# Gated linear attention in halves of 64 tokens with the state inside the output matmul, and a feed-forward block behind it

## The chip, the cores and the metric

The kernel runs on one core of a Trainium2 chip. A core has five engines that work side by side, each through its own instructions in order: PE (TensorE, matmuls, with its weight loads shown apart as PEld), DVE (VectorE), ACT (ScalarE), POOL (GpSimd) and SP (SyncE, which here issues DMAs). Matmuls write to PSUM; DVE and ACT can read it[...]. The metric is the time of one execution in microseconds on the device.

## The reference

There are 4 batches, 8 heads, 768 tokens and a head size of 48; d_model is 8 x 48 = 384. Everything is 32-bit floating point, except the two weight matrices, which arrive as 64-bit numbers.

```
state = alpha[t, :, None] * state + k[t] outer v[t]     # per batch and head, 48 x 48
y[t]  = q[t] @ state
x     = y, heads side by side                           # (4, 768, 384)
xn    = (x - mean(x)) / sqrt(var(x) + 1e-6) * g_ln
out   = x + max(xn @ w_ch1, 0) @ w_ch2                  # 384 -> 1536 -> 384
```

The recurrence runs over all tokens. In a block of tokens it can be written with matmuls. With L the running sum of log(alpha) from the block's start, q times exp(L) is matched against k times exp(-L), entries with a later key are cleared, and the result multiplies v. The state from before the block enters as (q times exp(L)) @ state. At the block's end the state is (state + (k exp(-L))^T v) times exp(L of the last token), here called the gate.

## The kernel before, in words

The tokens are cut in 6 chunks of 128; a chunk of one batch is a block, so there are 24 blocks. The generator `attention(c, b)` (L242) computes one block, step by step; each `yield` ends a turn. Its turns are:

- `la`, the logarithm on ACT (L246); `lps`, the running sum as a matmul with a triangle of ones (L249); two exponentials on ACT, `ek` and `eq` (L253, L254)
- k times `ek` on POOL (L256), q times `eq` on DVE (L258); a DMA writes the last row of `eq` to DRAM (`row`, L262), and a later one reads it back as a column per head (`gate`, L294)
- transposes of q and k on PE (`tps`, L272), copied out of PSUM to `qkT` by ACT or DVE (L276, L278); heads 2p and 2p+1 are a pair and sit in partitions 0 to 47 and 64 to 111
- scores `aps` (L285) on PE, copied to `at` by DVE with the triangle as mask (L289), so that cleared entries stay zero
- output `yps`: the scores times v (L307), and from the second chunk on q times the state, accumulated into the same place (L302); copied to `x` by ACT (L311) and kept in DRAM (L314)
- sums for the state, `sps` (L321), added to `st` by DVE (L326) and multiplied by the gate on POOL (L331)
- mean and variance on DVE (L335, L336), `rstd` on ACT (L338, L339), the normalised `xn` on DVE (L342), its transpose `xps` on PE (L349), copied to `xT` by ACT (L351)

The feed-forward part takes a chunk of all four batches together. Chunk 0 uses plain matmuls (`hidden`, L372, and `project`, L384). The other chunks use schemes that need fewer products and more sums: 15 products per half of the hidden layer (`hidden_product`, L612), with sums of inputs (`combine_x`, L588), and 20 products for the output (`product`, L455), with sums of hidden values (`combine_hidden`, L442). The sums of weights are made once on POOL: `combine_first` (L565) for the first matrix and `combine_weights` (L415) for the second. The weights come in 12 pieces of 768 KB; `take_weights` rounds each to 32 bits with DVE and ACT (L168 to L184). Gains `g_ln` are multiplied into the first matrix there.

The order of all this is written out: in the string `ORDER` each character is one turn. Letters a to x are the 24 blocks, A to L the weight pieces, M the feed-forward matmuls with what empties their PSUM tiles, S the sums of weights, X and N the sums of inputs and hidden values, R the rectifier, O loads of the kept `x`. Every engine gets its instructions in this order, so an instruction that waits holds all later ones of its engine.

All loads of attention and of weights are issued by SP (L121, L156). PSUM has three pools of tiles that matter: tag "a" with three buffers (`lps`, `tps`, `aps`), tag "s" with two (`yps`, `sps`, `xps`), tag "m" with three (feed-forward).

## Time and profile before

| | |
|---|---|
| three runs | 475.37, 476.41 and 476.61 us, median 476.41 |
| profiled execution, span | 472.3 us |
| that span below the median | 4.1 us |
| clock granted to TensorE | 1.000 |
| DMA | 43.29 MB, 92 GB/s in the mean |
| first hidden matmul (L372) | 47.31 us after the start |

The span runs from the first to the last instruction of the one execution that was profiled; what lies around it is not in it, so sums over rows are compared with 472.3 and not with the median. The page gives per engine the time it was busy and, per group of instructions, line, engine, operation, the tile written and the tiles read, the shapes, the number, the total and mean duration, and the idle time before with what ended it. A 32-bit matmul is two passes, so its group counts twice the calls in the code; a transpose is one. Durations of passes overlap: the mean of a row is longer than the distance from one to the next, and for PE's own rate the distance counts.

### The profile page before, as it was taken

How to read it: one execution, taken by the hardware profiler on the slowest of the kernel's cores; microseconds unless marked ns; L12 is line 12 of the kernel's file. 1: busy time of each engine (PE TensorE's matmuls, PEld its weight loads, DVE VectorE, ACT ScalarE, POOL GpSimd, SP SyncE). 2: the span in 40 equal slices, each digit the busy share in tenths (PEclk: the TensorE clock that was granted, in tenths of full speed). 3: DMA queues.
4: the chain of work that ended last, by engine and by line, in shares of the span. 5: the costliest groups of instructions: out<-in, count | busy, mean ns of one | idle time of the engine just before them, and what ended most of it. 6: DMA issues, size and time to landing. Idle time of an engine off the chain costs nothing.

```text
span 472.3 us, 9365 instructions
## 1 busy us (share of the span) xinstructions
PE 457.1 (97%) x3690; PEld 384.5 (81%) x3690; DVE 356.6 (76%) x662; ACT 152.9 (32%) x335; POOL 222.7 (47%) x222
## 2 busy tenths in 40 slices
PE   7899999999999999999999999999999999998996
PEld 5768465567688889998898998898998899987896
DVE  3799899867377799876788867688677579765673
ACT  4576354511033523124342121543031341223300
POOL 4142103069969990727461426460435360544513
PEclk9999999999999999999999999999999999999999
DMA  8986856403301422240331231330020110210001
GB/s 260 334 248 196 282 157 224 123 19 102 85 17 52 129 75 67 70 118 15 104 101 52 86 102 51 83 101 1 34 81 23 35 35 0 80 56 0 1 18 51
DMA packets 40132, 43.29 MB, mean 92 GB/s; under 512 B 13956, under 2 KB 36228, under 8 KB 40088
## 3 DMA queue, kind: packets, MB, share of 16 engines
q1 hardware_dynamic: 39544, 42.56, 29.4%
q8 instruction: 29, 0.48, 0.4%
q10 hardware_dynamic: 544, 0.13, 0.1%
q14 instruction: 15, 0.12, 0.1%
HBM read 33.20 MB, written 9.48 MB: 90 GB/s over the span
## 4 chain that ended last, share of the span: by engine, by line
PE 85%; DVE 5%; POOL 4%; ACT 2%; DMA 2%; issue 2%; POOLq 0%; DVEq 0%; ACTq 0%
PE ops L455 24%; PE hps L612 24%; PE hps L372 7%; PE ops L384 7%; PE aps L285 5%; PE yps L307 4%; PE tps L272 4%; PE yps L302 4%; PE lps L249 3%; PE sps L321 2%; PE xps L349 2%; DMA rk<-in_k_dram 1%; DVE at L289 1%; DVE sum L588 1%; DMA ra<-in_alpha_dram 1%
## 5 line engine op out<-in xcount | busy, mean ns | idle before, releaser
L471 POOL TENSOR_TENSOR ob<-ob,u 128x192 f32<-128x192 f32 x40 | 27.5, 699 | 83.3 <-DVE ob L468 63.9
L612 PE MATMUL hps<-sum,w 128*128 128x256 f32 x240 | 59.9, 382 | 1.1 <-DVE hT L655 1.1
L612 PEld LDWEIGHTS hps<-sum,w 128*128 128x128 f32 x240 | 44.7, 190 | 7.9 <-DVE hT L655 1.5
L455 PE MATMUL ops<-w,hT 128*128 128x192 f32 x280 | 49.6, 328 | 0.0
L664 ACT ACTIVATE hT<-hT 128x512 f32<-128x512 f32 x60 | 36.3, 628 | 35.6 <-POOL hT L634 21.3
L455 PEld LDWEIGHTS ops<-w,hT 128*128 128x128 f32 x280 | 45.7, 190 | 1.1
L331 POOL TENSOR_TENSOR st<-st,gate 128x384 f32<-128x384 f32 x20 | 19.1, 959 | 53.6 <-DVE st L326 44.3
L631 POOL TENSOR_TENSOR hT<-hT,u 128x512 f32<-128x512 f32 x10 | 12.9, 1287 | 56.9 <-DVE u L630 56.9
L256 POOL TENSOR_TENSOR qk<-rk,ek 128x384 f32<-128x384 f32 x22 | 23.3, 1059 | 30.0 <-PE sps L321 12.6
L307 PE MATMUL yps<-rv,at 128*64 128x48 f32 x768 | 36.5, 219 | 0.1
L289 DVE COPY_PREDICATED at<-consts,aps 128x512 f32<-128x512 int32 x48 | 32.2, 724 | 3.6 <-PE aps L285 3.2
L307 PEld LDWEIGHTS yps<-rv,at 128*64 128x64 f32 x768 | 32.9, 138 | 0.6 <-DVE at L289 0.3
L372 PE MATMUL hps<-xT,w 128*128 128x512 f32 x72 | 32.4, 597 | 0.0
L384 PE MATMUL ops<-w,hT 128*128 128x384 f32 x96 | 32.2, 488 | 0.0
L612 PE MATMUL hps<-xT,w 128*128 128x256 f32 x120 | 31.1, 382 | 0.9 <-DVE hT L644 0.9
L285 PE MATMUL aps<-qkT 48*128 48x128 f32 x384 | 28.6, 285 | 2.1 <-DVE at L289 1.3
L285 PEld LDWEIGHTS aps<-qkT 48*128 48x128 f32 x384 | 23.8, 187 | 8.0 <-issue 4.0
L302 PE MATMUL yps<-st,qkT 112*64 112x96 f32 x320 | 29.8, 257 | 0.0
L455 PE MATMUL ops<-ws,sum 128*128 128x192 f32 x160 | 28.9, 328 | 0.7 <-DVE sum L442 0.7
L455 PE MATMUL ops<-ws,hT 128*128 128x192 f32 x160 | 29.5, 327 | 0.0
L276 ACT COPY qkT<-tps 112x512 f32<-112x512 f32 x32 | 18.2, 597 | 29.0 <-PE tps L272 25.7
L455 PEld LDWEIGHTS ops<-ws,sum 128*128 128x128 f32 x160 | 26.3, 190 | 1.4 <-DVE sum L442 1.0
(141 smaller groups left out, 1020.9 us busy)
## 6 DMA issues: line engine op xcount, KB each, us to landing
ws<-in_moe_w_ch_dram SPq DMA_DIRECT2D x12, 768.0 KB, 6.1
ra<-in_alpha_dram SPq DMA_DIRECT2D x24, 192.0 KB, 2.6
rk<-in_k_dram SPq DMA_DIRECT2D x24, 192.0 KB, 3.4
rq<-in_q_dram SPq DMA_DIRECT2D x24, 192.0 KB
rv<-in_v_dram SPq DMA_DIRECT2D x24, 192.0 KB, 2.8
kept<-x SPq DMA_DIRECT2D x24, 192.0 KB, 1.9
ob<-kept SPq DMA_DIRECT2D x24, 192.0 KB, 2.9
out_dram<-ob SPq DMA_DIRECT2D x19, 192.0 KB, 1.9
```

The lines of the kernel that those rows point to most:

```text
L256: nc.gpsimd.tensor_mul(qk[:, 1, :, :D], raws.pop(("k", c, b)), ek)
L285: nc.tensor.matmul(aps[i][:, p], qkT[rows, 1, p], qkT[rows, 0, p], start=True, stop=True)
L289: nc.vector.copy_predicated(out=at[:, i], data=aps[i], mask=mask.unsqueeze(1).broadcast_to([P, NP, P]))
L302: nc.tensor.matmul(yps[s, p].rearrange("p a b -> p (a b)"), qkT[:, 0, p, s], sts[b][:R, p].rearrange("p a b -> p (a b)"), start=True, stop ...
L307: nc.tensor.matmul(yps[s, p, i], at[:, i, p, s], vt[:, 2 * p + i], start=(c == 0), stop=(c == 0 or i == 1))
L331: nc.gpsimd.tensor_mul(st, st, gate.unsqueeze(2).broadcast_to([P, NP, 2 * D]))
L372: nc.tensor.matmul(hps, w1[:, f, j * P:(j + 1) * P], xT_of[c][:, f], start=(f == 0), stop=(f == NF - 1))
L384: nc.tensor.matmul(ops_of[b], hT_of[c][:, j, b], w2[:, j], start=(j == 0), stop=(j == NJ - 1))
L455: nc.tensor.matmul(acc, lhs[:, j], rhs[:, j], start=(j == 0), stop=(j == NT - 1))
L471: getattr(nc.gpsimd, f"tensor_{op}")(x, x, y)
L612: nc.tensor.matmul(acc[:, i], w, b, start=True, stop=True)
L664: nc.scalar.activation(out=x, in_=x, func=AFT.Relu)
```

## The change

Attention works on a chunk of 128 tokens as two halves of 64, each with its own running sum (`upto` has two triangles on its diagonal). Heads p and p+4 form a pair. The scores are computed inside each half only (`aps`, 64 keys by 64 queries). They land in the 64 partitions of `at` that the transposed q of that head does not use; ACT copies q's transpose to the other ones (in two copies), and a separate `kT` holds k's. Beside v, the tile `va` holds the state in the partitions that match q's, so that one matmul per head and half gives scores times v plus q times state. `va` holds all of v in half tiles, and `rv` half of it a second time, in six loads for two batches. The sums for the state, `ups`, are made per half: DVE adds them, POOL multiplies by the half's gate (`gate` has two columns per pair), and ACT copies the state to the next half's place (`carry`, four small copies per block in all). The last chunk now needs a first half's sums and gate too.

exp(-L) is written back to PSUM, and k's product with it moves from POOL to DVE. The normalised `xn` moves from DVE to POOL. The gains are applied when `xT` is copied, in three copies with a scale per partition, and no longer in the weights. `combine_weights` moves from POOL to DVE and gets its own letter W. Loads of alpha, k, q and v take two batches at a time, those of k, q and v of the first chunk inside the blocks' turns; from the middle on `load_one` takes single blocks. Loads of weights go to ACT's queue, and the first three are issued in turns of their own. The string `ORDER` is another one; its extra letters at the end of a generator do nothing.

```diff
--- before.py
+++ after.py
...
-    "babdabcdcabadcbacabbdabaabacababdabacbdbccbadAccdddcBcCedfeacbacaeBeffcgbaededbe"
...
+    "aabBaaaaababbdbaaaabbbBddaaBaaAabbbacceacCdccaabbdbbbcceeeedfebbbaccccacdbAbdcAc"
...
-    raw = ctx.enter_context(tc.tile_pool(name="raw", bufs=B))
+    raw = ctx.enter_context(tc.tile_pool(name="raw", bufs=B // 2))
...
+    HS = P // 2
+    halves = [slice(HS * s, HS * s + HS) for s in range(2)]
...
-    upto = (r[None, :] >= r[:, None]).astype(np.float32)
+    upto = ((r[None, :] >= r[:, None]) & (r[None, :] // HS == r[:, None] // HS)).astype(np.float32)
...
-    def load(c, b, names="akqv"):
-        for n, src in (("a", alpha), ("k", k), ("q", q), ("v", v)):
...
-            t = raw.tile([P, H, D], FP32, name=f"r{n}", tag=f"r{n}",
...
-            nc.sync.dma_start(t, src[b, c * P:(c + 1) * P])
-            raws[n, c, b] = t
+    def load(c, m, names):
+        bs = range(2 * m, 2 * m + 2)
+        rows = slice(c * P, (c + 1) * P)
+        for n, src in (("a", alpha), ("k", k), ("q", q)):
+            if n in names:
+                t = raw.tile([P, 2, 2, NP, D], FP32, name=f"r{n}", tag=f"r{n}")
+                nc.sync.dma_start(t.rearrange("t b i p d -> t b (i p d)"),
+                                  src[bs.start:bs.stop, rows].rearrange("b t h d -> t b (h d)"))
+                raws.update({(n, c, b): t[:, b - bs.start] for b in bs})
+        if "v" in names:
+            rv = raw.tile([P, 2, NP, D], FP32, name="rv", tag="rv")
+            va = raw.tile([P, 2, 2, 2, NP, D], FP32, name="va", tag="va")
+            src = v[bs.start:bs.stop, rows].rearrange("b (s t) (i p) d -> i s t b (p d)", s=2, i=2)
+            for i in range(2):
+                nc.sync.dma_start(rv[halves[i]].rearrange("t b p d -> t b (p d)"), src[i, i])
+                for s in range(2):
+                    nc.sync.dma_start(va[halves[1 - i], :, s, i].rearrange("t b p d -> t b (p d)"),
+                                      src[i, s])
+            for b in bs:
+                raws["v", c, b] = rv[:, b - bs.start], va[:, b - bs.start]
+    lone = {}
+    def load_one(n):
+        c, b = divmod(n, B)
+        for n, src in (("a", alpha), ("k", k), ("q", q)):
+            if n not in lone:
+                lone[n] = raw.tile([P, 2, 2, NP, D], FP32, name=f"r{n}", tag=f"r{n}")
+            t = raws[n, c, b] = lone[n][:, b % 2]
+            nc.sync.dma_start(t.rearrange("t i p d -> t (i p d)"),
+                              src[b, c * P:(c + 1) * P].rearrange("t h d -> t (h d)"))
...
-    for names in ("a", "kq", "v"):
-        for b in range(B):
-            load(0, b, names)
+    for m in range(B // 2):
+        load(0, m, "a")
...
     def load_weights(i):
...
-        nc.sync.dma_start(dst, src)
+        nc.scalar.dma_start(dst, src)
     def round_weights(i):
...
-        if not gains:
-            stt(out=dst, in0=dst, scalar=2.0 ** -20, in1=hi.bitcast(FP32),
-                op0=AOP.mult, op1=AOP.mult)
-            return
-        for f in range(NF):
-            stt(out=dst[:, f], in0=dst[:, f], scalar=g20[:, f:f + 1],
-                in1=hi[:, f].bitcast(FP32), op0=AOP.mult, op1=AOP.mult)
+        stt(out=dst, in0=dst, scalar=2.0 ** -20, in1=hi.bitcast(FP32), op0=AOP.mult, op1=AOP.mult)
     def take_weights(i):
+        if i < STAGED:
+            load_weights(i)
+            yield
...
-        elif pieces[i][2]:
-            for f in range(NF):
-                nc.vector.tensor_scalar_mul(pieces[i][0][:, f], pieces[i][0][:, f],
-                                            g_col[:, f:f + 1])
...
-    for i in range(STAGED):
-        load_weights(i)
...
-    sts = [cpool.tile([P, NP, 2, D], FP32, name=f"st{b}") for b in range(B)]
+    sts = [cpool.tile([R, NP, D], FP32, name=f"st{b}") for b in range(B)]
...
-    ats = [cpool.tile([P, 2, NP, P], FP32, name=f"at{i}") for i in range(2)]
+    ats = [cpool.tile([P, NP, 2, 2, HS], FP32, name=f"at{i}") for i in range(2)]
...
     def attention(c, b):
-        qk = qk_of(c, b).rearrange("p i a b c -> p i (a b) c")
-        eq = eq_of(c, b).rearrange("p a b c -> p (a b) c")[:, :, :D]
-        la = work.tile([P, H, D], FP32, name="la", tag="la")
+        if c == 0 and b % 2 == 0:
+            load(0, b // 2, "kq")
+            yield
+            load(0, b // 2, "v")
+            for i in range(2):
+                for d in range(2):
+                    nc.gpsimd.memset(raws["v", 0, b + d][1][halves[i], 0, i], 0.0)
+            yield
+        qk = qk_of(c, b).rearrange("t n p i c -> t n i p c")[:, :, :, :, :D]
+        eq = eq_of(c, b).rearrange("t p i c -> t i p c")[:, :, :, :D]
+        la = work.tile([P, 2, NP, D], FP32, name="la", tag="la")
...
-        lv = lps[:, :DM].rearrange("p (h d) -> p h d", d=D)
-        ek = work.tile([P, H, D], FP32, name="ek", tag="ek")
-        nc.scalar.activation(out=ek, in_=lv, func=AFT.Exp, scale=-1.0)
+        lv = lps[:, :DM].rearrange("t (i p d) -> t i p d", i=2, d=D)
...
-        yield
-        nc.gpsimd.tensor_mul(qk[:, 1, :, :D], raws.pop(("k", c, b)), ek)
-        yield
-        nc.vector.tensor_mul(qk[:, 0, :, :D], raws.pop(("q", c, b)), eq)
-        if c + 1 < NCB:
-            row = dram.tile([1, NP, P], FP32, name="row", tag="row")
-            gate = work.tile([P, NP], FP32, name="gate", tag="gate", bufs=B)
-            nc.sync.dma_start(row, eq_of(c, b)[P - 1:P].rearrange("o a b c -> o a (b c)"))
-        yield
-        n = c * B + b + (B if c < 2 else B // 2)
-        if c < 2 or 3 * B <= n < NCB * B:
-            load(*divmod(n, B), "akq")
-        yield
-        qkT = work.tile([R, 2, NP, P], FP32, name="qkT", tag="qkT", bufs=2)
+        nc.scalar.activation(out=lv, in_=lv, func=AFT.Exp, scale=-1.0)
+        yield
+        nc.vector.tensor_mul(qk[:, 1], raws.pop(("k", c, b)), lv)
+        yield
+        nc.vector.tensor_mul(qk[:, 0], raws.pop(("q", c, b)), eq)
+        row = dram.tile([2, NP, P], FP32, name="row", tag="row")
+        gate = work.tile([P, 2, NP], FP32, name="gate", tag="gate", bufs=B)
+        nc.sync.dma_start(row, eq_of(c, b)[HS - 1::HS].rearrange("o a b c -> o a (b c)"))
+        yield
+        n = c * B + b + 2
+        if c < 2 and b % 2:
+            load(c + 1, b // 2, "akq")
+        elif n == 3 * B + 1:
+            load_one(n - 1)
+            load_one(n)
+        elif 3 * B + 1 < n < NCB * B:
+            load_one(n)
+        yield
+        at = ats[b % len(ats)]
+        kT = work.tile([R, NP, 2, HS], FP32, name="kT", tag="kT", bufs=2)
+        rows = [slice(0, 64), slice(64, R)]
...
-            if i == 0 or c < 2:
-                nc.scalar.copy(out=qkT[:, i], in_=tps)
+            tv = tps.rearrange("r p (s t) -> r p s t", s=2)
+            if i == 0:
+                for j in range(2):
+                    nc.scalar.copy(out=at[rows[j], :, j], in_=tv[rows[j]])
...
-                nc.vector.tensor_copy(out=qkT[:, i], in_=tps)
-            yield
-        at = ats[b % len(ats)]
-        aps = [ps.tile([P, NP, P], FP32, name=f"aps{i}", tag="a", bufs=3) for i in range(2)]
+                (nc.vector.tensor_copy if c == 0 else nc.scalar.copy)(out=kT, in_=tv)
+            yield
+        aps = [ps.tile([P, NP, 2, HS], FP32, name=f"aps{i}", tag="a", bufs=3) for i in range(2)]
+        for p in range(NP):
+            for s in range(2):
+                for i in range(2):
+                    rs = slice(64 * i, 64 * i + D)
+                    nc.tensor.matmul(aps[i][halves[1 - i], p, s], kT[rs, p, s], at[rs, p, i, s],
+                                     start=True, stop=True)
+        yield
+        for i in range(2):
+            h = halves[1 - i]
+            nc.vector.copy_predicated(
+                out=at[h, :, i], data=aps[i][h],
+                mask=mask[h, h].unsqueeze(1).unsqueeze(1).broadcast_to([HS, NP, 2, HS]))
+        yield
+        with nc.allow_non_contiguous_dma(reason="two rows to columns"):
+            nc.sync.dma_start(gate, row.rearrange("o a c -> c o a"))
+        yield
+        rv, va = raws.pop(("v", c, b))
+        heads = [slice(0, 64), slice(64, R)]
+        last = c + 1 == NCB
+        ups = [ps.tile([R, NP, D], FP32, name=f"ups{s}", tag="s") for s in range(1 if last else 2)]
+        for p in range(NP):
+            for s, up in enumerate(ups):
+                for i, h in enumerate(heads):
+                    vs = rv[halves[s], p] if s == i else va[halves[s], s, i, p]
+                    nc.tensor.matmul(up[h, p], qk_of(c, b)[halves[s], 1, p, i, :h.stop - h.start],
+                                     vs, start=True, stop=True)
+        yield
+        st = sts[b]
+        def carry(s, to):
+            for i, h in enumerate(heads):
+                nc.scalar.copy(out=to[h, s, i], in_=st[h])
+        for s, up in enumerate(ups):
+            nc.vector.tensor_add(st, up, st)
+            yield
+            nc.gpsimd.tensor_mul(st, st, gate[:R, s].unsqueeze(2).broadcast_to([R, NP, D]))
+            yield
+            if s == 0:
+                carry(1, va)
+                yield
+        yps = ps.tile([P, 2, NP, D], FP32, name="yps", tag="s")
...
-                rows = slice(64 * i, 64 * i + D)
-                nc.tensor.matmul(aps[i][:, p], qkT[rows, 1, p], qkT[rows, 0, p],
-                                 start=True, stop=True)
-        yield
-        for i in range(2):
-            nc.vector.copy_predicated(out=at[:, i], data=aps[i],
-                                      mask=mask.unsqueeze(1).broadcast_to([P, NP, P]))
-        yield
-        if c + 1 < NCB:
-            with nc.allow_non_contiguous_dma(reason="one row to columns"):
-                nc.sync.dma_start(gate, row.rearrange("o a c -> c (o a)"))
-        yield
-        vt = raws.pop(("v", c, b))
-        yps = ps.tile([P, NP, 2, D], FP32, name="yps", tag="s")
-        sides = [slice(64 * s, 64 * s + 64) for s in range(2)]
-        for p in range(NP):
-            if c > 0:
-                for s in sides:
-                    nc.tensor.matmul(yps[s, p].rearrange("p a b -> p (a b)"), qkT[:, 0, p, s],
-                                     sts[b][:R, p].rearrange("p a b -> p (a b)"),
-                                     start=True, stop=False)
-            for i in range(2):
-                for s in sides:
-                    nc.tensor.matmul(yps[s, p, i], at[:, i, p, s], vt[:, 2 * p + i],
-                                     start=(c == 0), stop=(c == 0 or i == 1))
+                rs = slice(0, P if i == 0 else R)
+                for s in range(2):
+                    nc.tensor.matmul(yps[halves[s], i, p], at[rs, p, i, s], va[rs, s, i, p],
+                                     start=True, stop=True)
...
-        nc.scalar.copy(out=x, in_=yps.rearrange("p a b d -> p (a b d)"))
+        nc.scalar.copy(out=x, in_=yps.rearrange("t a b d -> t (a b d)"))
+        yield
+        if not last and b % 2:
+            load(c + 1, b // 2, "v")
+        yield
+        if not last:
+            carry(0, raws["v", c + 1, b][1])
...
-        yield
-        if c + 1 < NCB:
-            sps = ps.tile([R, NP, D], FP32, name="sps", tag="s")
-            heads = list(enumerate((slice(0, 64), slice(64, R))))
-            for p in range(NP):
-                for i, s in heads:
-                    nc.tensor.matmul(sps[s, p], qk_of(c, b)[:, 1, p, i, :s.stop - s.start],
-                                     vt[:, 2 * p + i], start=True, stop=True)
-        yield
-        if c + 1 < NCB:
-            for i, s in heads:
-                nc.vector.tensor_add(sts[b][s, :, i], sps[s], sts[b][s, :, i])
-        yield
-        if c + 1 < NCB:
-            load(c + 1, b, "v")
-            st = sts[b].rearrange("p a b d -> p a (b d)")
-            nc.gpsimd.tensor_mul(st, st, gate.unsqueeze(2).broadcast_to([P, NP, 2 * D]))
...
+        yield
...
-        nc.vector.tensor_scalar(out=xn, in0=x, scalar1=mv[:, 0:1], scalar2=rstd,
+        nc.gpsimd.tensor_scalar(out=xn, in0=x, scalar1=mv[:, 0:1], scalar2=rstd,
...
-        nc.scalar.copy(out=xT_of[c][:, :, b], in_=xps)
+        for f in range(NF):
+            nc.scalar.mul(xT_of[c][:, f, b], xps[:, f], g_col[:, f:f + 1])
...
-        add, sub = nc.gpsimd.tensor_add, nc.gpsimd.tensor_sub
+        add, sub = nc.vector.tensor_add, nc.vector.tensor_sub
...
-        new = [(raw.tile([P, H, D], FP32, name=f"r{n}", tag=f"r{n}", bufs=B)
-                .rearrange("p h d -> p (h d)"), extra[:, 2 * i + k])
+        spare = {n: raw.tile([P, 2, 2, NP, D], FP32, name=f"r{n}", tag=f"r{n}") for n in "akq"}
+        new = [(spare[n][:, k].rearrange("t i p d -> t (i p d)"), extra[:, 2 * i + k])
...
-    turns |= {"M": mlp(), "S": sums(), "R": relus(),
+    turns |= {"M": mlp(), "S": combine_first(), "W": combine_weights(), "R": relus(),
```

## The prediction

> **What bounds the kernel now.** I read the page from the top: first the busy times and the slices, then the windows, then the weights of single runs of matmuls.
>
> ```profile
> span 472.3 us, 9365 instructions
> PE 457.1 (97%) x3690; PEld 384.5 (81%) x3690; DVE 356.6 (76%) x662; ACT 152.9 (32%) x335; POOL 222.7 (47%) x222
> ```
>
> The reader is to see that only PE has no room. The answer by windows (columns: PE, weight load, DVE, ACT, POOL, clock, DMA share, GB/s) says where this fails:
>
> ```profile
> 0.00:47.30 47.30, 40.72 (x523) 31.97 (x523) 35.89 (x72) 28.48 (x65) 16.44 (x23) 1.00 0.84 259
> 47.30:89.20 41.90, 41.90 (x264) 22.75 (x264) 38.84 (x64) 18.82 (x36) 6.73 (x7) 1.00 0.65 207
> 89.20:127.10 37.90, 37.90 (x209) 23.96 (x208) 23.24 (x37) 7.11 (x14) 28.48 (x37) 1.00 0.21 69
> 127.10:409.00 281.90, 280.59 (x2403) 254.96 (x2403) 218.98 (x414) 86.25 (x198) 143.88 (x127) 1.00 0.21 63
> ```
>
> At 47.3 the first hidden matmul (L372) starts. Up to there DVE and the DMA set the pace: DVE is busy 35.9 us and starts its real work only at 9.6, so 34 of 37.7 us are full, and the DMA engines are 84% busy. From 47.3 to 409 PE is without a gap. So two things count: how much PE work there is, and when the first hidden matmul can start. What a matmul costs is the time to the next kind's start, in the timeline of PE (start, duration), first with a state (last tokens but one block), then without (first 128 tokens):
>
> ```profile
> 366.34 1.16 PE L285 MATMUL aps<-qkT 48*128 48x128 f32 x16
> 367.44 0.39 PE L302 MATMUL yps<-st,qkT 112*64 112x96 f32 x4
> ...
> 369.17 0.48 PE L612 MATMUL hps<-xT,rq 128*128 128x256 f32 x1
> ```
> ```profile
> 33.62 1.14 PE L307 MATMUL yps<-rv,at 128*64 128x48 f32 x32
> 34.69 0.55 PE L349 MATMUL xps<-consts,xn 128*128 128x128 f32 x3
> ```
>
> Scores take 1.10 us, the output with the state 369.17 - 367.44 = 1.73, without it 1.07. The chain of waits adds the rest:
>
> ```profile
> 36.77 0.59 PE sps L321 x14
> 213.01 0.65 PE lps L249 x2
> 147.64 5.18 PE hps L612 x24
> ```
>
> **What the Trainium skill says.** (1) "TensorE: Matmul & The Clock Gate", Part 3: matmuls whose tiles lie in other row and column strips of the array run at the same time. The trace agrees for each direction alone: the 16 of L285 alternate row strips and need 69 ns each, though one weight load lasts 187; the 32 of L307 alternate column strips, 33 ns each. Both at once, as the change has it, no run here shows. (2) "ScalarE: Activation LUTs", What ACT_TABLE_LOAD costs: an operand per partition adds about 93 ns. The trace agrees: L338 with one 295 ns, L339 without 203. (3) "GPSIMD Engine Reference", 4.1 Engine selection: one-input work runs there at about line rate, two-input at half of VectorE's. No one-input row of this size is in the trace. (4) "DMA: Bandwidth & Descriptors", Queues, rings and completion order: a DMA engine takes turns between the rows of SP and of ACT. All loads here are SP's, so the trace can't say.
>
> **The change part by part.** Block means 128 tokens of one batch; there are 24.
>
> *PE.* A block now costs 0.65 (lps) + 0.87 (8 transposes of 109 ns) + 1.10 (aps) + 1.07 or 1.73 (yps) + 0.57 (sps) + 0.33 (xps): 4.59 for the first 4, 5.25 for 16, 4.68 for the last 4 (no sps), together 121.1 us. With 600 x 0.216 (L612), 800 x 0.1625 (L455), 72 x 0.43 (L372), 96 x 0.3225 (L384) = 321.6, PE has 442.7 us.
> The 16 state passes of L302 go: the transposed q and the state fill rows that the scores no longer need, so yps is 32 passes as in L307, 1.07. Blocks with a state: 20, so 20 x 0.66 = 13.2 us gained.
> Scores: 32 passes of 64 columns in place of 16 of 128. Bounds: 0.88, the rate of eight of L307 (219 ns), and 1.8, if opposite tiles don't overlap at all. I take 1.0: 24 x 0.1 = 2.4 us gained.
> Sums for the state (ups): 32 passes in place of 16, in four tiles instead of two. Bounds 0.5 (twice the rate) and 1.18 (the rate of L321). I take 0.7, and 0.35 for the last four, which had none: 20 x 0.13 + 4 x 0.35 = 4.0 us lost.
> Sum: 13.2 + 2.4 - 4.0 = **11.6 us less**; block by block, 4.62 for 20 blocks and 4.27 for 4 make 109.5 against 121.1. Ends: scores +2.9 or -19, sums +4.4 or -10.6, so from 19 us less to 18 more.
>
> *DVE.* Gains k's product (24 x 0.56, by L388, which also reads PSUM) = 13.4 and the weight sums (13 x 1.1, L442's 0.81 for 512 elements scaled to 768; bounds 0.86 to 1.2) = 14.3, one state add per half (+1.5); loses the normalisation (24 x 0.587 = 14.1), 16 qkT copies less 4 (8.2) and split gains (1.8): +5, 76% to 77%. As a total it bounds nothing. But by the turns of the two orders, DVE's share between the first hidden matmul and the first product of the next 128 tokens grows from 57 to 75 us of row durations, while PE has 79: rounding and weight sums now fall there, and evacuations that PE waits for (three PSUM buffers) stand behind them. Consecutive DVE instructions overlap by some 7% (rows sum to 382, busy 356.6), so I charge nothing; if that cover fails, it is 2 to 4 us.
>
> *ACT.* One more transposed copy (24 x 0.6), k's copy in 12 more blocks (7.2), carries (four copies by 20 and two by 4, at L474's 0.32: 28), xT in three scaled pieces (24 x 0.5 by point 2): 153 to about 215 us, 46%. The 12 weight issues at 0.4 to 0.5 go there too, 5 us. Cover: PE's own work between the turns; behind a carry that waits stand the next block's Ln and Exp, and behind those PE's lps.
>
> *Buffers.* The lps tile in PSUM is now freed by DVE's product, not by ACT's Exp, and three such buffers serve transposes and scores too; the two sums of a block hold both small PSUM buffers until DVE has added them. From sums to output the state goes through DVE (0.36), POOL (0.6), ACT (0.64) and their semaphores, some 2.5 us. The new order puts 2.7 to 4.1 us of PE work between them in the first four blocks and 3.5 to 30 in the others, so it is hidden except where one of the three queues is behind.
>
> *POOL.* Loses k's product (25.6) and the weight sums (24.9); gains the normalisation (24 x 0.45 to 1.06, I take 0.7) and smaller but more gate products (44 x 0.6 against 19.1): about 27 less.
>
> *SP and DMA.* v is read one and a half times: +2.4 MB, at the start's 259 GB/s 9 us of transfer if all fell there; 2 of 12 pairs do, so 1.5. Six v issues per pair at 0.38. A gate is two rows, 1024 elements; 13956 packets under 512 B fit in the DMA share now, so latency alone counts: row out, row in, then POOL, then the carry on ACT, then yps.
>
> *The start.* I added these durations over the turns ahead of the first M: before PE 31, DVE 44, ACT 34; after 25.5, 36 and 35. DVE's 34 us become 34 x 36/44 = 28, at the same density 31, from 9.5: first hidden matmul at 40.5. Against it: SP's loads for the next 128 tokens wait for k's and q's products and stand ahead of the k and q of batches 2 and 3. About 3.3 MB and two weight pieces (1.6 MB) have to move first: 4.9 MB at 259 to 330 GB/s is 15 to 19 us. The product of k for d then waits until about 19, while DVE has only some 8 us of other work from 9.5: 2 us lost. The first carry waits for a gate at about 17, which holds ACT's Ln of c: 2 us; the tail of stats, POOL, transposes and three xT copies: 2. So 46.5.
>
> **The sum.** After the first hidden matmul PE has 442.7 - 31 = 411.7 us now, and 472.3 - 47.3 - 411.7 = 13.3 idle, mostly the last two stages, which stay. After the change 431.1 - 25.5 = 405.6. Span = 46.5 + 405.6 + 13.3 = 465.4. The profiled span is 4.1 below the median of the runs, 476.4; I carry that: **469.5**, called 470.
>
> **The rivals.** *B, the start shrinks as DVE's work does* (41), and the small tiles overlap better by 3 us: 41 + 402.6 + 13.3 + 4.1 = 461. For it: DVE's 36 against 44. Against: the DMA share of 0.84.
> *C, the tiles don't overlap enough* and eat the state passes: PE within 2 us of now beyond the start, 476.
> *D, slower: the start becomes a chain of transfers.* Place: ACT and DVE queues ahead of the first M, behind gates, k and q of the second pair, and v for the carries. The time is the first hidden matmul plus 423, so it decides at 53.4 us. Five or six waits of 2 to 3 us in a row make it 59: 482. For it: three of the engines now wait on each other inside each block, while no large matmul is there to hide it. Against: PE and DVE have less to do there.
>
> **Chances.** The likeliest 0.5 (its own range 464 to 475), B 0.17, C 0.08, D 0.25. Range 459 to 483: B's far end and D's are left out. A measurement can tell 0.3%, 1.4 us: faster 0.66, same 0.09, slower 0.25.
>
> **What would show it.** No 96-column passes; yps of 32 in about 1.07 everywhere; aps at 1.0, ups at 0.7; DVE near 362, ACT near 215, POOL near 195; first hidden matmul at 46.5; PE without a gap from there to the last two stages. Wrong if that start is past 53, if aps is near 1.8, or if PE waits for DVE in the stage of the first products, where the new order puts seven X sums in a row (4 us).

## The result and the profile after

The changed kernel took 490.85 us in the median of four runs (489.3 to 492.79), the kernel before 476.31 us beside it: a ratio of 1.0325, with a 95% interval of 1.0285 to 1.0364. Forecast were 470 us in a range of 459 to 483. The change made the kernel 3.2% slower. The spans of the two profiled executions differ by 17.7 us and the medians by 14.5, because the one of the kernel before lies 4.1 us below its median (another of its executions, of 476.56 us, shows a clock of 0.993 in place of 1.000) and the one of the kernel after 0.9 below, so the windows below show a loss some 3 us too large.

The top of the page of the kernel after:

```profile
span 490.0 us, 10513 instructions
...
PE 454.5 (93%) x4138; PEld 374.9 (77%) x4138; DVE 355.7 (73%) x655; ACT 216.1 (44%) x507; POOL 225.6 (46%) x240
...
PEclk9779899999999999999999999999999999999999
```

PE is busy for 2.6 us less than before in a span that is 17.7 us longer, and its clock is below full in the first slices; in the profiled execution before it was full throughout. Next the answer by windows, cut at the first hidden matmul (L418, at 58.43 us; before L372, whose first pass starts at 47.24), at the last one and at the first product of chunk 1 (L658; before L612). The kernel after has four lines, the kernel before three, since its two middle ones are taken together. Columns: length, PE, weight load, DVE, ACT, POOL, clock, DMA share, GB/s.

```profile
0.00:58.43 58.43, 38.72 (x546) 28.72 (x547) 36.06 (x70) 34.19 (x82) 15.62 (x30) 0.86 0.81 213
58.43:98.38 39.95, 39.95 (x348) 21.29 (x347) 35.47 (x49) 21.15 (x38) 10.70 (x12) 1.00 0.64 182
98.38:145.71 47.33, 43.56 (x318) 26.83 (x317) 35.14 (x52) 19.59 (x50) 26.83 (x28) 0.96 0.27 79
145.71:490.00 344.29, 332.29 (x2929) 298.11 (x2927) 248.99 (x487) 141.15 (x338) 172.43 (x171) 1.00 0.23 65
```
```profile
0.00:47.24 47.24, 40.66 (x523) 31.91 (x523) 35.83 (x72) 28.48 (x65) 16.44 (x23) 1.00 0.84 259
47.24:126.91 79.67, 79.67 (x472) 46.59 (x471) 61.95 (x100) 25.93 (x49) 35.02 (x44) 1.00 0.45 142
126.91:472.30 345.39, 336.74 (x2699) 305.98 (x2697) 258.78 (x492) 98.44 (x221) 171.26 (x156) 1.00 0.19 57
```

So 11.2 us are lost ahead of the first hidden matmul, 7.6 between it and the first product, and 1.1 are won in all that follows. PE without work: 6.6 us before and 19.7 after in the start, 8.7 and 15.8 behind it. DVE, in the start, was busy for 35.8 us before and 36.1 after, and without work for 11.4 and 22.4.

The passes themselves came out as forecast. Pieces of the chain of waits (start, length, passes; of the 32 passes of `ups` in the last line 25 lie on the chain):

```profile
217.59 1.07 PE yps L362 x32
...
286.24 1.08 PE aps L320 x32
...
299.69 0.60 PE ups L340 x25
```

No pass has 96 columns any more, the output takes 1.07 for a block, the scores 1.08 and the sums for the state 0.60.

What filled the start, from the same view (start, length; a DMA's piece is a wait for its landing):

```profile
4.21 9.27 DMA ws<-in_moe_w_ch_dram
...
18.23 7.87 DMA rk<-in_k_dram
...
26.20 0.56 DVE more L283
26.90 1.62 PE lps L277 x2
...
34.78 5.82 DMA gate<-row
40.74 0.52 POOL st L352
41.27 0.35 ACT va L347
...
42.10 0.36 DVE st L350
...
43.98 0.78 DVE qk L285
...
54.07 0.73 DVE at L325
...
55.42 1.28 PE lps L277 x2
```

A weight piece, k of the second pair and a gate follow each other, and behind the last of them the state goes from POOL over ACT to DVE. (`more` is the tile of k's product for the third block.) From 42.1 to 54.8 us the chain then stays on DVE: by the windows DVE was busy for 18.8 of the 20.0 us from 34.8 to 54.8, after it had waited 7.8 us for k, which the kernel before has no wait for. So its work came late. The running sum `lps`, 0.65 to 0.84 us at full clock, takes 1.62 and 1.28. The windows show why:

```profile
0.00:17.50 17.50, 10.72 (x104) 8.33 (x104) 8.46 (x22) 8.54 (x15) 3.65 (x14) 1.00 0.71 200
17.50:31.50 14.00, 6.59 (x81) 4.20 (x82) 4.90 (x11) 2.96 (x7) 1.85 (x6) 0.51 0.99 267
31.50:55.00 23.50, 17.97 (x362) 14.28 (x359) 20.03 (x35) 19.99 (x51) 8.73 (x10) 1.00 0.82 209
55.00:58.43 3.43, 3.43 (x10) 1.91 (x10) 2.66 (x4) 2.69 (x10) 1.39 (x1) 0.53 0.46 96
```

The clock was at half from 17.5 to 31.5, from 55 to 58.5 and, not shown, from 133.5 to 137 us, each time after a stretch in which PE waited. The Trainium skill, "TensorE: Matmul & The Clock Gate", Part 1, states a window of about 3.4 us whose activity sets the clock, half after an idle window. The lengths of 14.0, 3.5 and 3.5 us fit such a window; that it must be idle does not: in the 3.5 us ahead of each fall PE was busy for 1.4, 1.2 and 1.3. PE's busy time in each, times what the clock lacks to 1, is an estimate of what was lost to the clock: 3.2 + 1.6 + 1.6 = 6.4 us.

One group on POOL is far from its forecast (line, operation, tiles, count, then busy us and mean ns):

```profile
L387 POOL TENSOR_SCALAR xn<-x,mv,rstd 128x384 f32<-128x384 f32 x24 | 43.7, 1821 | 47.0 <-ACT rstd L384 29.0
```

PE's wait for it (us in total, times, longest), after and then before:

```profile
PE xps L394 <- POOL xn L387: 5.8, 5, 2.2
```
```profile
PE xps L349 <- DVE xn L342: 0.2, 1, 0.2
```

All five fall behind the first hidden matmul, where PE's time without work grew by 7.1 us.

### The profile page after: what moved, and what is told of

It reads as the page before. It is cut to its first block, busy times and chain, and to the rows that moved or that the text cites. A ratio compares the mean times of both kernels' runs of the same rounds, so it can differ in the third digit from the quotient of the medians.

```text
span 490.0 us, 10513 instructions
## 1 busy us (share of the span) xinstructions
PE 454.5 (93%) x4138; PEld 374.9 (77%) x4138; DVE 355.7 (73%) x655; ACT 216.1 (44%) x507; POOL 225.6 (46%) x240
## 4 chain that ended last, share of the span: by engine, by line
PE 62%; DVE 15%; POOL 10%; DMA 7%; issue 3%; ACT 2%; SPq 0%; POOLq 0%; DVEq 0%; ACTq 0%
PE ops L501 23%; PE hps L658 20%; PE yps L362 3%; DMA ws<-in_moe_w_ch_dram 3%; PE hps L418 3%; PE lps L277 3%; POOL xn L387 3%; PE aps L320 3%; DVE at L325 2%; PE tps L305 2%; PE ups L340 2%; PE ops L430 2%; DMA rk<-in_k_dram 2%; DVE w L209 2%; PE xps L394 2%
## 5 line engine op out<-in xcount | busy, mean ns | idle before, releaser
L352 POOL TENSOR_TENSOR st<-st,gate 112x192 f32<-112x192 f32 x44 | 27.1, 620 | 110.7 <-DVE st L350 65.1
L387 POOL TENSOR_SCALAR xn<-x,mv,rstd 128x384 f32<-128x384 f32 x24 | 43.7, 1821 | 47.0 <-ACT rstd L384 29.0
L658 PE MATMUL hps<-sum,w 128*128 128x256 f32 x240 | 59.3, 382 | 1.9 <-DVE hT L701 1.1
L658 PEld LDWEIGHTS hps<-sum,w 128*128 128x128 f32 x240 | 44.4, 190 | 9.2 <-DVE hT L701 1.5
L325 DVE COPY_PREDICATED at<-consts,aps 64x512 f32<-64x512 int32 x48 | 35.2, 733 | 7.2 <-PE aps L320 5.8
L347 ACT COPY va<-st 64x192 f32<-64x192 f32 x88 | 30.5, 347 | 21.9 <-POOL st L352 20.5
L311 ACT COPY at<-tps 64x512 f32<-64x512 f32 (+1 forms) x48 | 27.7, 578 | 11.7 <-PE tps L305 11.2
L320 PEld LDWEIGHTS aps<-at,kT 48*64 48x64 f32 x768 | 25.2, 138 | 9.6 <-issue 4.4
L418 PE MATMUL hps<-xT,w 128*128 128x512 f32 x72 | 32.5, 599 | 0.0
L397 ACT ACTIVATE xT<-xps,small 128x128 f32<-128x128 f32 x72 | 20.9, 370 | 26.1 <-PE xps L394 25.9
L658 PE MATMUL hps<-xT,w 128*128 128x256 f32 x120 | 31.7, 387 | 0.6 <-DVE hT L690 0.6
L320 PE MATMUL aps<-at,kT 48*64 48x64 f32 x768 | 28.7, 225 | 2.3 <-DVE kT L313 2.0
L362 PEld LDWEIGHTS yps<-va,at 112*64 112x64 f32 (+1 forms) x768 | 24.3, 138 | 6.9 <-issue 4.0
L277 PE MATMUL lps<-la,consts 128*128 128x384 f32 x48 | 23.2, 575 | 6.9 <-DVE more L283 6.4
L677 POOL TENSOR_TENSOR hT<-hT,u 128x512 f32<-128x512 f32 x10 | 12.7, 1271 | 36.1 <-DVE u L676 36.0
```

The lines of the kernel that those rows point to most:

```text
L277: nc.tensor.matmul(lps[:, :DM], tri, la, start=True, stop=True)
L311: nc.scalar.copy(out=at[rows[j], :, j], in_=tv[rows[j]])
L320: nc.tensor.matmul(aps[i][halves[1 - i], p, s], kT[rs, p, s], at[rs, p, i, s], start=True, stop=True)
L325: nc.vector.copy_predicated(out=at[h, :, i], data=aps[i][h], mask=mask[h, h].unsqueeze(1).unsqueeze(1).broadcast_to([HS, NP, 2, HS]))
L347: nc.scalar.copy(out=to[h, s, i], in_=st[h])
L362: nc.tensor.matmul(yps[halves[s], i, p], at[rs, p, i, s], va[rs, s, i, p], start=True, stop=True)
```

## The experiments

In the table, H0 is the first hidden matmul, "to product" the time from there to the first product, "rest" what follows, all from the profiled execution; ratios are against runs of the kernel before beside each kernel. Where intervals overlap by much, as those of e5 to e7 with that of after, the difference is not told from noise.

| kernel | H0 | to product | rest | median us | ratio (95%) |
|---|---|---|---|---|---|
| before | 47.2 | 79.7 | 345.4 | 476.31 | 1 |
| after | 58.4 | 87.3 | 344.3 | 490.85 | 1.0325 (1.0285 to 1.0364) |
| e1_xn_dve | 60.3 | 89.2 | 346.3 | 498.88 | 1.0492 (1.0466 to 1.0517) |
| e2_loads_first | 61.0 | 87.6 | 344.4 | 494.60 | 1.0401 (1.0372 to 1.0430) |
| e3_xn_loads | 65.3 | 87.8 | 346.3 | 500.90 | 1.0530 (1.0485 to 1.0575) |
| e4_weights_sp | 56.3 | 86.0 | 344.6 | 486.52 | 1.0238 (1.0201 to 1.0274) |
| e5_loads_then_weights | 59.0 | 84.3 | 344.3 | 488.46 | 1.0284 (1.0219 to 1.0350) |
| e6_gate_of_ones | 59.8 | 87.2 | 344.2 | 489.22 | 1.0315 (1.0227 to 1.0403) |
| e7_light_rounding | 57.9 | 85.9 | 344.2 | 488.36 | 1.0280 (1.0211 to 1.0350) |
| e8_xn_act | 61.7 | 87.0 | 344.4 | 496.08 | 1.0437 (1.0323 to 1.0550) |
| e9_filled_gaps | 62.1 | 84.6 | 344.4 | 491.14 | 1.0353 (1.0304 to 1.0402) |
| e10_later_rounding | 57.5 | 84.8 | 344.5 | 488.39 | 1.0286 (1.0240 to 1.0332) |
| e11_later_rounding_filled | 55.6 | 83.6 | 344.2 | 485.23 | 1.0228 (1.0184 to 1.0273) |
| e12_filled_ones | 53.8 | 83.4 | 344.4 | 481.67 | 1.0148 (1.0112 to 1.0185) |
| e13_row_by_act | 58.6 | 84.5 | 346.0 | 490.45 | 1.0321 (1.0274 to 1.0367) |
| e14_weight_sums_pool | 56.5 | 91.4 | 347.7 | 501.10 | 1.0543 (1.0491 to 1.0595) |
| e15_old_order | 93.3 | 95.2 | 409.4 | 601.73 | 1.2658 (1.2600 to 1.2716) |
| e16_old_order_new_engines | 93.3 | 96.5 | 408.4 | 599.56 | 1.2640 (1.2557 to 1.2724) |
| e17_old_order_ones | 85.0 | 93.5 | 405.5 | 586.19 | 1.2326 (1.2298 to 1.2353) |
| e18_second_v_later | 54.6 | 84.0 | 344.5 | 484.35 | 1.0180 (1.0145 to 1.0216) |

**The engine of the normalised x, and the loads.** The first four kernels undo one part each: `xn` on DVE again (e1), the loads of k, q and v of chunk 0 ahead of the order (e2), both (e3), the weights issued by SP (e4).

```diff
-        nc.gpsimd.tensor_scalar(out=xn, in0=x, ...
+        nc.vector.tensor_scalar(out=xn, in0=x, ...
```


> The changed kernel with the normalised xn computed on DVE again, nothing else. Theory POOL (xn at 1.8 us on POOL, in front of other POOL work and PE's transposes, costs 10 us or more of the loss): 478 to 482 us, with fewer waits of xps for xn, and POOL busy near 182 us. Theory START (the loss is the late first hidden matmul and late weights, xn is hidden): 489 to 491. Theory DVE (DVE is what is short from 60 to 120 us): slower than 491, since DVE gets 14 us more.


```diff
-    for m in range(B // 2):
-        load(0, m, "a")
+    for names in ("a", "kq", "v"):
+        for m in range(B // 2):
+            load(0, m, names)
```


> The changed kernel with k, q and v of the first 128 tokens of all four batches issued ahead of the order, as the kernel before did it, instead of inside the turns of blocks a and c. Theory START: the wait of DVE for k (7.8 us) and PE's wait behind it (6.4) go, the first hidden matmul comes at 50 to 53 instead of 58.6, and the time is 482 to 486. Theory DMA (the transfers are limited by bandwidth, whatever their order): the wait moves to the first weight piece or to the gate, first hidden matmul 57 or later, 489 to 492.

> Both of the two edits together. If START and POOL are separate costs, their gains add: 470 to 477. If one hides the other, about the better of the two alone.


```diff
-        nc.scalar.dma_start(dst, src)
+        nc.sync.dma_start(dst, src)
```


> The changed kernel with the weight pieces issued by SP again, at the same turns. Theory QUEUE (weights on ACT's row take DMA turns from the loads of attention, and the first piece took 9.3 us to land): loads of k for batches 2 and 3 land earlier, the time falls by 3 to 8 us. Theory START without that (the order of SP's issues is the cause): unchanged within 2 us, or slower by up to 5 us as SP waits for staging buffers.

Moving `xn` back cost 8 us more, in all three stretches, though on DVE it takes 0.65 us and on POOL 1.82. So the slow operation was still better where it was. PE waited for `xn` longer than on POOL, 11.8 us in total; no run makes `xn` cheaper where it stands, so how much of the loss its price is stays open. Loads ahead of the order made the start longer: the first weight piece still landed ahead of v, at 14.2 us, SP waited 5.7 us for it before it went on with its issues of v, and the v that the chain then waits for landed at 22.8. e3, both together, was the slowest of the four. Only SP for the weights helped, by 4 us: the first row went out at 9.5 in place of 13.6 us, k of the second pair at 15.1 in place of 18.2, and PE's wait for k's product fell from 6.4 to 1.7 us. That is what QUEUE expected; whether it was the sharing of the DMA engines or a wait of SP's (last section) the run can't tell. The theories POOL and START both missed; DVE had the sign of e1 right, and e7 below tests it.

**Weights behind the loads, and single suspects.** e5 joins e2 and e4, so that the transfers come in the order of before. e6 puts ones in place of the gate in the first halves of chunk 0's blocks, so it leaves the decay out there; e7 leaves out three of the six operations that round a weight piece; e8 puts `xn` on ACT.

> Loads of k, q and v of chunk 0 ahead of the order, and the first weights issued by SP, so that they come behind all 24 loads of chunk 0 as in the kernel before. If the start is long because transfers come late in the wrong order (TRANSFERS), the first hidden matmul moves from 58.4 to about 50 us, and the time falls to 482 to 485. If the start is set by the round trip of the gate and by DVE's turns (GATE), the first hidden matmul stays at 56 to 60 and the time at 487 to 492.


```diff
+            g = ones if c == 0 and s == 0 else gate
-            nc.gpsimd.tensor_mul(st, st, gate[:R, s]...
+            nc.gpsimd.tensor_mul(st, st, g[:R, s]...
```


> The first half of chunk 0 multiplies the state by a column of ones in place of the gate, so its state waits for no transfer; the gate is still written and read, and the second half still uses it. Part of the computation is so left out. GATE: the first hidden matmul comes 4 to 8 us earlier (50 to 54), time 482 to 487. TRANSFERS: under 2 us earlier, time 488 to 491, as the next late transfer or DVE's backlog takes its place.


```diff
-        ts(out=lo, in0=hi, scalar1=0x7FF00000, scalar2=None, op0=AOP.bitwise_and)
...
-        stt(out=hi, in0=hi, scalar=-(1 << 31), in1=lo, ...
-        stt(out=dst, in0=dst, scalar=2.0 ** -20, in1=hi.bitcast(FP32), ...
+        stt(out=dst, in0=dst, scalar=2.0 ** -20, in1=dst, ...
```


> Three of the six operations that round a weight piece are left out (two of DVE, 1.4 us a piece and more beside a busy POOL, and ACT's one), so the weights' exponents and signs are wrong; loads, matmuls and order are the same. If DVE's backlog with weights holds the stage from the first hidden matmul to the first product (DVE), that stage shrinks from 87.3 us to about 80, what PE needed before (79.7), and the time falls to 480 to 484, a part of it in the start. If POOL with the normalised x is what holds it (POOL), it stays at 85 to 87 us and the time at 487 to 490.


```diff
+        nc.vector.tensor_scalar_mul(nm, mv[:, 0:1], -1.0)
...
-        nc.gpsimd.tensor_scalar(out=xn, in0=x, scalar1=mv[:, 0:1], scalar2=rstd, ...
+        nc.scalar.activation(out=nm, in_=nm, func=AFT.Copy, scale=rstd)
+        nc.scalar.activation(out=xn, in_=x, func=AFT.Identity, bias=nm, scale=rstd)
```


> The normalised x on ACT, as rstd times x plus a bias, which takes DVE one and ACT one small extra operation each; 24 x 1.82 us leave POOL and come to neither POOL nor DVE in their size. POOL: the stage after the last hidden matmul shrinks by 3 to 5 us and later stages by 3 or so, time 482 to 486. DVE: the chain only changes its last link, time 487 to 491; above 491 if ACT's place in order now holds x back.

None moved the first hidden matmul forward by more than 0.6 us. For e5 that is what GATE expected, for e6 what TRANSFERS did: each theory is met where the other's wait was taken away. e7 took 23 us of work from DVE (355.7 to 332.7) and won 2.5, which the intervals do not tell from nothing. Behind the first hidden matmul 19.9 us of it fell in the stretch to the first product, and that stretch shrank by 1.4: there DVE's load is not the bound. In the start it took only 2.9 us away, too little to say the same. On ACT `xn` took 0.71 us, PE waited for it 7.5 us, and the kernel was some 5 us slower than after, as DVE expected in case ACT held `xn` back. What PE waited for longest in the start, by the waits of four kernels (total us, times, longest): after, then e6, e5 and e10, which is told below:

```profile
PE lps L277 <- DVE more L283: 6.4, 1, 6.4
```
```profile
PE lps L279 <- DVE more L285: 10.0, 1, 10.0
```
```profile
PE tps L304 <- DVE at L324: 8.4, 1, 8.4
```
```profile
PE lps L276 <- ACT la L273: 8.0, 1, 8.0
```

Each has one wait of 6 to 10 us, and not for the same thing. After: DVE holds k's product until k of the second pair has landed, and with it the PSUM tile that the next `lps` needs. With ones for the gate the same landing is later still. With the loads in order DVE stands at the rounding of a weight piece that lands at 19.5 us, ahead of the masked copy. With that moved, ACT stands at a state's copy that waits for the gate, ahead of the next logarithm. Taking one wait away uncovers the next, in these four kernels.

**Clock and place.** e9 puts matmuls on constants, whose result nobody reads, ahead of five waits, e10 moves two turns of the first weight piece in e5's kernel, e11 does both, with 6 such matmuls for 14 at the first place.

```diff
+    def warm(n, out=None):
+        if out is None:
+            out = ps.tile([P, 512], FP32, name="hps", tag="m", bufs=3)[:, :2 * P]
+        for _ in range(n):
+            nc.tensor.matmul(out, tri, consts[:, :out.shape[1]], start=True, stop=True)
...
+        if (c, b) == (0, 2):
+            warm(14)
...
```


> Matmuls on constants, whose result nobody reads, stand ahead of the five places where PE waits for 1 to 6.4 us in the kernel after (27 in the start, 8 short ones ahead of the last transposes of chunk 1's normalised x). In the kernel after the granted clock is 0.5 from 17.5 to 31.5, from 55 to 58.5 and from 133.5 to 137 us, in the kernel before it is 1.0 all through. If half of the loss is PE running at half clock because it waited (CLOCK), the clock stays at 1.0, the first hidden matmul comes 3 to 5 us earlier (53 to 55) and the first product 5 to 7 earlier: time 483 to 486. If the waits themselves are what counts and PE's slow passes lie in their shadow (WAITS), the clock is 1.0 as well but only the last stretch ahead of the first hidden matmul shortens: 1 to 2 us, time 488 to 490.


```diff
-    "aabBaaaaababbdbaaaabbbBddaaBaaAabbbacceacCdccaabbdbbbcceeeedfebbbaccccacdbAbdcAc"
+    "aabBaaaaababbdbaaaabbbddaaaaAabbbacceacCdcBcaabbdbBbbcceeeedfebbbaccccacdbAbdcAc"
```


> The loads-then-weights kernel (488.5), with two turns of the order moved: the first rounding of the first weight piece comes after the second block's scores and after the third block's running sum, not ahead of the second block's masked copy, where DVE waited for a landing at 19.5 us. If a DVE instruction that stands in the order ahead of what is ready is the cause of the long start (PLACE), PE's wait of 8.4 us before the second block's transposes goes and the first hidden matmul comes 4 to 7 us earlier (52 to 55), time 481 to 485. If the gate or another chain is as late (OTHERS), under 2 us, time 486 to 488.5.

> Both: the order with the later rounding, and matmuls on constants in the gaps. CLOCK and PLACE together: the first hidden matmul at 49 to 52, time 477 to 481. If only one of them counts, no more than 1 us better than the better of the two kernels.

In e9 the half clock only came later, from 37 to 50.5 us, and the start grew to 62.1; both theories had expected a clock of 1.0 (window of e9):

```profile
37.00:50.50 13.50, 12.72 (x185) 10.75 (x183) 8.78 (x18) 8.78 (x21) 3.18 (x4) 0.50 0.82 216
```

The stretch up to the first product fell from 87.3 to 84.6; with the fill ahead of the last transposes the clock was at full in all of it. e10 alone kept the start within 1 us of after, as OTHERS expected. Together with the later rounding, where no long wait is left behind the fills, the clock is low for 3.5 us only, and both stretches shrink: 55.6 and 83.6. e11 is 3.2 us faster than e10, from which it differs by the fills alone; its slowest run is faster than the fastest of e10. The forecast of 477 to 481 for the two together was not reached (485.2).

**What is left in the start.** All but e14 change e11. e12 adds ones for the gate, as e6 did; e13 has ACT issue the row's DMA directly behind the exponential; e18 leaves the second pair's v at its old turn, so that SP comes to the row earlier. e14 changes the kernel after and belongs to the other open point: it puts the second weights' sums on POOL.

> The kernel with loads first, later rounding and filled gaps (485.2), with the column of ones for the first half of chunk 0 in place of the gate; so part of the computation is left out. In the trace of that kernel the row and two gates take 13.7 us of the 55.6 up to the first hidden matmul. GATE: with the other late things out of the way the gate is what is left; the first hidden matmul comes at 47 to 51, time 477 to 481. OTHERS: another chain is as long, as it was in the kernel after, where ones changed nothing; the first hidden matmul at 54 to 56, time 484 to 486.


```diff
+        nc.scalar.dma_start(row, eq_of(c, b)[HS - 1::HS].rearrange("o a b c -> o a (b c)"))
         nc.scalar.activation(out=lv, in_=lv, func=AFT.Exp, scale=-1.0)
```


> The same kernel without the ones; the gate's row is written by a DMA of ACT's queue directly behind the exponential that makes it, ahead of the other exponential, and no longer by SP behind twelve loads of v and the first weights. GATE: the row goes out at about 9 in place of 16.4 us and the first gate lands 3 to 5 us earlier; the first hidden matmul 1 to 4 us earlier, time 481 to 484. OTHERS: no change within 1 us.


```diff
-        add, sub = nc.vector.tensor_add, nc.vector.tensor_sub
+        add, sub = nc.gpsimd.tensor_add, nc.gpsimd.tensor_sub
```


> The kernel after with the 13 sums of the second weights (13 x 1.1 us on DVE) on POOL again. If DVE's load counted (DVE), 2 to 4 us faster than after (486 to 488); if POOL's with the normalised x counts (POOL), 1 to 5 us slower (491 to 496).

> The kernel with loads first, later rounding and filled gaps (485.2), with the six loads of v of the second pair not ahead of the order but at the third block's second turn, so that SP comes to the first row and gate some 3.6 us earlier. GATE in SP's queue: the row goes out at 12 to 13 in place of 16.4 us, the first hidden matmul 1 to 3 us earlier, time 482 to 484.5. OTHERS: no change within 1 us.

With the other waits shorter the gate counts: e12 is 3.6 us faster than e11, where ones alone (e6) had won nothing that can be told; it came out between what GATE and OTHERS expected. 53.8 us is still 6.6 later than before; the fills in the start take 8.8 us of PE's time there, how much of it in gaps was not measured, and the remainder was not resolved to a single link. e18 sent the row out at 11.5 in place of 16.4 us and gained 1.0 at H0 and 0.9 in the median, less than the intervals can tell apart. e13 lost 5 us, which neither theory had. Its first row went out at 8.0, but SP came to the issue that reads it back only at 20.0 (20.5 in e11), and that gate landed at 26.7 in place of 24.8: so the early row gained nothing. Besides, each of the 24 issues holds ACT, the longest for a microsecond, and the share of either in the 5 us is open (20 of the 24; columns after the count: shortest, median, longest ns, first and last start):

```profile
L289 ACTq DMA_DIRECT2D row<-eq x20: 459/460/1051, 8.0 to 355.7; - x20
```

e14 was 10 us slower than after, more than the 1 to 5 that POOL expected. In this kernel the move of the second weights' sums to DVE was right.

**The new attention in the old order.** e15 has every turn of the new attention where the old order had the one that it stands for, with `xn` on DVE, the second weights' sums on POOL, and the loads and first weights issued by SP ahead of it; where a buffer had to be free first, the turns that free it were drawn ahead. e16 has the new engines, e17 is e15 with ones for every gate, so it leaves the decay out.

```diff
-    "aabBaaaaababbdbaaaabbbBddaaBaaAabbbacceacCdccaabbdbbbcceeeedfebbbaccccacdbAbdcAc"
+    "ABCaaccbabdabcdbcaadcbacabbdabaabacababdabacbdaaaababaccbbbbbdAccdddcBcCedfecabc"
...
```


> The new attention, turn for turn, in the order string of the kernel before: each old turn gives the new turns that stand for it (the state's sums, the gate and its copies come where the output's matmuls stood, the output's matmuls where the old state's sums stood), loads of chunk 0 and the first weights ahead of it by SP, the normalised x on DVE and the weights' sums on POOL as before. If the attention itself is the gain and the new order is where it was lost (ORDER), PE has some 10 us less work than before and few waits: first hidden matmul at 42 to 49, time 463 to 472. If the attention in halves brings waits of its own, for the gate above all (HALVES), the first hidden matmul comes at 50 or later and the time is 476 to 492.

> The same, with the normalised x on POOL and the weights' sums on DVE as in the kernel after. ORDER: within 5 us of the other kernel, slower for the normalised x's 1.6 to 1.8 us on POOL. HALVES: as late at the first hidden matmul as the other one.


```diff
+            g = ones
```


> The new attention in the old order (601.7), with a column of ones in place of every gate; the gates are still written and read, nobody waits for them, and the decay of the state is left out. If the gate's round trip through DRAM is what the attention in halves waits for when the order gives it no room (GATE), the time falls by 60 us or more, to under 540. If it is the chain of engines itself (sums on PE, add on DVE, product on POOL, copies on ACT, output on PE, one behind the other) that the old order has no room for (CHAIN), it falls by less than 40, to 560 or more.

601.7 us, and with the new engines the same within the intervals: the old order has no room for the new attention, and both theories missed by over 100 us. PE was without work for 97.8 us of the span (15.2 before), and its granted clock was 0.89 in the mean, so slow passes are a part of it too. The two largest waits of PE in e15, then in e17:

```profile
PE ups L337 <- DVE st L347: 25.7, 9, 11.6
PE yps L359 <- ACT va L344: 17.8, 11, 5.0
```
```profile
PE ups L339 <- DVE st L349: 15.0, 9, 4.5
PE yps L362 <- ACT va L346: 14.9, 11, 4.6
```

Without any wait for a gate the time falls by 15.5 us, and most of the waits stay: sums for the next block stand behind DVE's add, the output behind ACT's copy. That is what CHAIN expected: in this order the hand-offs within a half (PE, DVE, POOL, ACT, PE) need room more than the gate does. The turns that had to be drawn ahead are part of the 601.7, and how much was not measured.

No version with the new attention beat the kernel before. The fastest that computes all of it, e18, is 1.8% slower.

## Why the prediction was wrong, by its own steps

- **The start: 46.5 predicted, 58.4 measured.** This step failed, by 11.9 us, in two terms. The first is "34 x 36/44 = 28" for DVE. The 44 counts all that the order puts ahead of the first M, 84 instructions by the two orders; but the kernel before had begun only 72 of them when its first hidden matmul started. In the new order 69 stand ahead of it, and by then all were done. So DVE had as much to do as before, 36.1 us for 35.8. The second is the three waits at 2 us each. DVE was without work for 11.0 us more than before, with 7.8 for k, 2.6 for weight pieces and 2.1 for copies of the state among its waits, none of which it had before. The wait for k of the second pair, put at 2, was 7.87 on the chain, and the one for the gate, put at 2, was 5.82 for one landing, and 8.0 at PE where it came first (e10). PE had less to do there and waited 13.1 us longer. Taken away singly the waits gave little, so they do not add up; chains of nearly one length fit that, and the last 6.6 us (e12) were not resolved.
- **PE's saving: 11.6 predicted.** The sizes of the passes were right (scores 1.08 for 1.0, output 1.07, sums 0.60 for 0.7), and so was attention's saving. Counted by the distance from each matmul's start to the next one's in the traces, attention behind the first hidden matmul took 88.6 us before and 82.3 after: 6.3 less, for 6.1 predicted (411.7 to 405.6). But the feed-forward matmuls, as many as before, took 327.3 and 333.5, of which 1.6 is the clock. The other 4.6 us are longer distances, not split here into changes of kind and waits that overlapping records hide. By the windows PE's work there fell from 416.4 to 415.8, 414.2 without the loss to the clock: 2.2 us.
- **"13.3 idle, which stay": failed.** Behind the first hidden matmul PE had 8.7 us without work before (the windows count as work some of what the prediction called idle) and 15.8 after. Of the 7.1 us more, 5.6 are the waits for `xn`, which the prediction put at nothing there. The difference of the spans closes with these: 11.2 (start) + 7.1 (idle) + 1.6 (clock) - 2.2 (work) = 17.7 us. In the prediction's own terms, 405.6 + 13.3 = 418.9 from the first hidden matmul on came out as 431.6, and the 4.1 us carried from span to median as 0.9.
- **DVE: "I charge nothing", 2 to 4 if the cover fails.** The stretch to the first product grew by 7.6: 3.8 of waiting, 1.6 of clock and 2.2 of matmuls that the new order places there. Of e7's 19.9 us less on DVE only 1.4 came back. PE waited there 1.4 us for a rounding and 2.2 for `xn`, so not the sum of DVE's rows broke the cover. That sum was close for the whole kernel: 355.7 for 362; ACT 216.1 for 215.
- **POOL: 27 less predicted, 3 more measured.** The term is `xn`, put at 0.7 (bounds 0.45 to 1.06) and measured at 1.82. It lies outside the bounds. The prediction weighed it as load on POOL, which had room, and not as a link that PE waits for (5.8 us). By e1 and e8, DVE and ACT were no better place for it in this order.
- **Rival D** named the place and nearly the time of the first hidden matmul (59), and with its chance of 0.25 it is the case that came. Its mechanism, transfers one behind the other, is half of it: the chain shows them, but e5 put the transfers in order and the start stayed. What D lacked is the stretch behind, 79.7 us to 87.3, so its 482 was 9 too low. B and C are refuted: the start did not shrink, and opposite tiles do overlap (scores 1.08 us, where no overlap would have been 1.8).

## What to carry to other kernels

Work saved on the busiest engine counts only where that engine is the bound; here, ahead of the first large matmul, nothing of it did, and what mattered was how long the engines waited for hand-offs and landings before they could do their share. A sum over what an order puts ahead of a point is not what an engine has done when another reaches that point. Where several chains of nearly one length end together, taking one away shows little: try them together before calling any of them innocent. And an order written out by hand belongs to the chains it was written for: when a change makes a chain longer, look for what will stand behind its waits on each engine's queue, and for PE falling to half clock after them. An operation that moves to an engine with room still needs a look at who waits for its result.

## What was not expected of the hardware

- The clock. In e9 it stayed at half for 13.5 us while PE was busy for 12.72 of them, though the Trainium skill, "TensorE: Matmul & The Clock Gate", Part 1, has it released after one busy window of 3.4 us. All of these were attention's matmuls; why they didn't release the clock is open. In the kernel after it rose at 31.5, after 3.5 us in which PE was busy throughout, as the page has it.
- One input is no guarantee of speed on POOL. The Trainium skill, "GPSIMD Engine Reference", 4.1 Engine selection, puts one-input work at about line rate; with two operands per partition 128 x 384 took 1.64 us undisturbed, more than the 1.06 of a product of two such tiles in the kernel before. DVE took 0.65 (mean in e1), ACT 0.71 (e8).
- DVE and POOL slow each other. The page's 1. Specifications says that they share their way to SBUF, with contention for DVE instructions of two inputs. In the chain of waits of the kernel after, a rounding step on DVE with POOL at rest and then at work, and `xn` on POOL with DVE at work and then at rest:

```profile
85.94 0.97 DVE w L201
...
92.19 2.11 DVE w L201
...
117.28 3.34 POOL xn L387
...
131.84 1.64 POOL xn L387
```

- SP waited for landings of DMAs that ACT had issued, with its own next issue ready (waits of the kernel after):

```profile
SPq L288 <- DMA ws<-in_moe_w_ch_dram: 7.7, 2, 5.0
```

The first gate's row went out at 13.57 us, just after the first weight piece had landed (13.48). In e2 it was an issue of v that waited so, for 5.7 us. In e4, where SP issues the weights itself, such waits sum to 0.4 us and the row went out at 9.45. The releaser is inferred from semaphores, and e4 changes the queue along with it, so what this wait alone costs is open.
